# A planned order for attention and two MLPs on one core: fitted delays, backward passes, and the softmax bias moved to GpSimd

## The chip, the cores and the metric

One Trainium2 chip, one of its cores. The time is the device time of one execution in microseconds (us), the median of three runs. The engines are named as in the profile: PE (matrix multiply; PEld loads its stationary operand), DVE (VectorE), ACT (ScalarE), POOL (GpSimd), SP (here only the issuer of all the DMAs).

## What is computed

```python
mask = q_bucket[:, :, :, None] == k_bucket[:, :, None, :]   # 6 sign bits of q@proj and k@proj
scores = scale * np.matmul(q, k.transpose(0, 1, 3, 2))
scores = np.where(mask, scores, -1000000000.0)
scores = scores - np.max(scores, axis=-1, keepdims=True)
attn = np.exp(scores)
attn = attn / (np.sum(attn, axis=-1, keepdims=True) + 1e-09)
x = np.matmul(attn, v)                  # 2 batches, 8 heads, 768 x 64; then to 1536 x 512
h = x @ moe_w_in; g = np.maximum(h, 0.0) ** 2; x = g @ moe_w_out          # 512 -> 2048 -> 512
h = x @ moe2_w_in; g = np.maximum(0.01 * h, h); out = g @ moe2_w_out
```

The weights and inputs are of higher precision than one pass of PE keeps, so each product is made of three matmuls on a high and a low half of each operand (`three`), and much of the work of DVE, ACT and POOL is the making of these halves.

## The kernel before, in words

**Attention.** For each of the two batches there are 48 slots: four pairs of heads, two heads each, six blocks of 128 queries (`attention`, `slot`). A slot is a chain. PE makes the scores of 128 queries against 768 keys into PSUM with four matmuls (L712). DVE goes over them once, with a floor that stands for the mask, copies them to SBUF (tile `e`) and takes the row maximum with `accum_out` (L733; the trace shows this as a TENSOR_SCALAR_CACHE_REDUCE and a DVE_READ_ACCUMULATOR). Before, the maximum is written into an unused column of the same PSUM bank. From it a bias for exp is made, 128 x 1 numbers (tile `sm`): the maximum times a scale plus a constant. It is made by DVE (L739) or by ACT (L742), as the planner chooses. ACT takes exp in place (L745). Then `e` becomes a high half (ACT L774 or DVE L775) and a low half (POOL L778 or DVE L779), which a DMA transposes (L792); or, for every second slot of batch 0, PE transposes `e` into PSUM (L756), and ACT and DVE make the halves from there (L764, L767). PE sums with v (L813 to L815), DVE and ACT divide (L837 to L853).

The bank of scores (key `("s", r)`) is free for the next scores when its last reader is done. Before, that reader is the bias, as it reads the maximum out of the bank. Batch 0 turns over three such banks, which also hold PE's transposes; batch 1 has one, the other PSUM being used by the MLP. `e` has four buffers in batch 0 and two in batch 1.

**MLP.** The first layer of batch 0 (`group`, `up`, `down`) is put among the slots of batch 1. The first layer of batch 1 and the second layer of both follow it alone (`alone`, `quad`, which makes the up products with seven block products in place of eight; `down`). Weights are fetched as 64-bit numbers (`wide`), converted by three DVE instructions (L988, L992, L995), kept in DRAM as fp32 for the second use and halved (ACT L1009 or DVE L1010; POOL L1014).

**The order.** Nothing is scheduled by the framework: every step is handed to `Plan.do` with a due time, what it reads and writes, and one or more engines with a cost in us each (its choice of engines is ordered: the first is the preferred one). `Plan.order` then plays the steps through, engine by engine, in time order: of the steps that are ready on an engine it takes the one with the smallest due time, unless a step that prefers another engine would end sooner there (within MARGIN). A step is ready when what it depends on has ended, plus a delay: LAG between engines, LAND after a DMA, ISSUE before one. A cost marked `Port`, and every cost of POOL, takes a resource named `port`, one at a time: the SBUF access that DVE and POOL share. `weighed` mixes the due time that the kernel's text gives with one from the longest chain behind the step (OWN is the share of the former). The instructions are then issued on each engine's in-order queue in the order of the played times, and semaphores follow from the data. All DMAs go through the one queue of SP in that order. The due times come from constants (PITCH, MAX_AT, FETCH, ...).

Of the kernel before, what the change touches and what calls it, by code (L numbers as in the profile page):

```python
# [27 lines left out]
class Plan:  # L28
# [59 lines left out]
    def order(self):  # L88
        steps = self.weighed()
        left = [len(after) for _, after, _, _ in steps]  # L90
        users = [[] for _ in steps]
        for n, (_, after, _, _) in enumerate(steps):
            for a in after:
                users[a].append(n)
# [3 lines left out]
        end = {}  # L98
# [3 lines left out]

        def offer(n):
            _, after, ways, since = steps[n]
            for e in ways:
                t = since
                for a in after:
                    at, on = end[a]
                    if on == e:
                        lag = self.SAME.get(e, 0.12)  # L110
                    else:
                        lag = (self.LAND if on == "dma" else self.LAG) + (self.ISSUE if e == "dma" else 0.0)
                    t = max(t, at + lag)
                heapq.heappush(late[e], (t, n))
# [4 lines left out]
        while len(end) < len(steps):  # L119
# [40 lines left out]
            cost = steps[n][2][e][0]  # L160
# [10 lines left out]
        return [(n, e, t) for t, _, n, e in sorted(placed)]  # L171
# [3 lines left out]
def lsh_attention_moe_moe_kernel(  # L175
# [1423 lines left out]
```

## Time and profile before

| | us |
|---|---|
| median of 3 runs | 797.35 (792.97 to 799.29) |
| the profiled execution's own time | 799.07 |
| its span, first to last instruction | 797.3 |
| PE busy | 697.5, 87% of the span |
| DVE busy | 633.4, 79% |
| ACT busy | 501.7, 63% |
| POOL busy | 257.6, 32% |
| mean granted clock of PE, as a share of 2.4 GHz | 0.959 |

The span divides by what PE is doing: attention of batch 0 until about 156 us, then a hand-over until 182 in which the MLP's first products begin; attention of batch 1 with the first MLP layer of batch 0 until about 384; a second hand-over until about 435; then the MLP alone to the end. The profile's busy times are sums of durations. On DVE and ACT the next instruction may start some hundredths of a microsecond before the last has ended, so the distance between starts is a little less than a duration. A wait is written "engine line <- engine tile line: us, times, longest".

### The profile page before, as it was taken

The page shows a single profiled execution, that of the slowest core. Times are in us where ns is not written, and L with a number is a line of the kernel's source. Part 1 is how long each engine was busy: PE and PEld are TensorE (multiplying, and loading weights), DVE is VectorE, ACT ScalarE, POOL GpSimd, SP SyncE. Part 2 cuts the span into 40 slices and gives each one's busy share as a digit, 9 for nine tenths or more (in the row PEclk, how much of TensorE's full clock was granted, in tenths as well). Part 3 has the DMA queues.
Part 4 walks back from the last instruction along what each step waited for, and adds up shares of the span by engine and source line. Part 5 has one row for each costly group of instructions (what it writes and reads, how often), then busy time and mean ns, then how long its engine had stood idle before and what let it go on. Part 6 is the DMA issues. An engine that isn't in the chain of part 4 may idle for free.

```text
span 797.3 us, 14295 instructions
## 1 busy us (share of the span) xinstructions
PE 697.5 (87%) x5408; PEld 545.5 (68%) x5408; DVE 633.4 (79%) x1304; ACT 501.7 (63%) x938; POOL 257.6 (32%) x207
## 2 busy tenths in 40 slices
PE   3686757579996895899997999999899999999998
PEld 2474545478895794698973788787567666676776
DVE  7889898968888779799889987788988578567332
ACT  4888688648678569666869875554766545434320
POOL 2332234223445335634436842311121123012000
PEclk9899999869999898799999999999999999999999
DMA  3467778697999999998821241213123304201012
GB/s 119 89 157 153 211 147 153 124 254 146 224 246 199 177 230 178 243 239 196 187 80 61 73 131 55 80 53 106 30 77 106 106 1 138 74 0 54 14 53 92
DMA packets 185861, 100.81 MB, mean 126 GB/s; under 512 B 149440, under 2 KB 171968, under 8 KB 185792
## 3 DMA queue, kind: packets, MB, share of 16 engines
q1 hardware_dynamic: 185792, 99.90, 52.8%
q8 instruction: 42, 0.69, 0.4%
q14 instruction: 27, 0.22, 0.1%
HBM read 51.38 MB, written 11.53 MB: 79 GB/s over the span
## 4 chain that ended last, share of the span: by engine, by line
PE 67%; DVE 18%; DMA 5%; issue 4%; ACT 4%; POOL 0%; SPq 0%; DVEq 0%; ACTq 0%; POOLq 0%
PE acc L1075 19%; PE acc L1077 19%; PE acc L1076 19%; PE s L712 4%; DVE ep L733 3%; DMA wide<-in_moe_w_in_dram 2%; DVE xb L544 1%; PE av L813 1%; PE av L815 1%; PE av L814 1%; DMA rawk<-in_k_dram 1%; DVE lo L733 1%; DMA tt<-xb 1%; DMA part<-ep 1%; DVE xb L616 1%
## 5 line engine op out<-in xcount | busy, mean ns | idle before, releaser
L778 POOL TENSOR_TENSOR ep<-ep 128x768 f16<-128x768 f32 x30 | 50.6, 1686 | 85.2 <-ACT ep L774 74.2
L745 ACT ACTIVATE ep<-ep,sm,scs 128x768 f32<-128x768 f32 x60 | 61.6, 1027 | 22.3 <-DVE sm L739 19.8
L1075 PE MATMUL acc<-xa,wi 128*128 128x384 f32 x192 | 71.0, 370 | 0.0
L1075 PE MATMUL acc<-g,wo 128*128 128x384 f32 x192 | 69.4, 361 | 0.0
L1075 PE MATMUL acc<-xb,tt 128*128 128x384 f16 x192 | 63.8, 332 | 6.1 <-ACT xb L1022 2.3
L1077 PE MATMUL acc<-xb,tt 128*128 128x384 f16 x192 | 63.8, 332 | 2.5 <-DVE tt L1027 2.5
L1305 DVE TENSOR_TENSOR part<-acc,part 128x384 f32<-128x384 f32 (+1 forms) x66 | 38.5, 589 | 34.5 <-PE acc L1077 34.3
L1077 PE MATMUL acc<-xa,wi 128*128 128x384 f32 x192 | 65.9, 343 | 0.0
L1076 PE MATMUL acc<-xa,wi 128*128 128x384 f32 x192 | 65.7, 342 | 0.0
L1076 PE MATMUL acc<-g,wo 128*128 128x384 f32 x192 | 64.8, 337 | 0.0
L1077 PE MATMUL acc<-g,wo 128*128 128x384 f32 x192 | 64.8, 337 | 0.0
L1156 ACT ACTIVATE acc<-acc,small 128x384 f32<-128x384 f32 x48 | 26.5, 551 | 60.8 <-PE acc L1077 60.1
L1076 PE MATMUL acc<-xb,tt 128*128 128x384 f16 x192 | 63.5, 331 | 0.7 <-DVE xb L1027 0.7
L1014 POOL TENSOR_TENSOR wo<-w,wo 128x512 fp32r<-128x512 f32 x29 | 41.5, 1444 | 57.9 <-ACT wo L1009 31.8
L1014 POOL TENSOR_TENSOR wi<-w,wi 128x512 fp32r<-128x512 f32 x26 | 35.3, 1361 | 65.0 <-ACT wi L1009 63.1
L733 DVE TENSOR_SCALAR_CACHE_REDUCE ep<-s 128x768 f32<-128x768 f32 x48 | 45.8, 954 | 12.5 <-PE s L712 9.3
L1053 POOL TENSOR_TENSOR rawk<-w 128x256 f32<-128x256 f32 x15 | 13.7, 914 | 114.5 <-DVE tt L1027 78.1
L995 DVE SCALAR_TENSOR_TENSOR w<-wide,w 128x512 int32<-128x512 int32 x64 | 49.3, 775 | 0.3
L1075 PEld LDWEIGHTS <-tt 128*128 128x128 f16 x288 | 28.3, 98 | 29.4 <-issue 12.9
L1166 DVE TENSOR_TENSOR g<-acc,g 128x384 fp32r<-128x384 f32 x68 | 37.0, 549 | 12.3 <-ACT g L1161 12.3
L992 DVE SCALAR_TENSOR_TENSOR w<-wide,w 128x512 int32<-128x512 int32 x64 | 46.5, 733 | 0.4
L712 PE MATMUL s<-xb 128*128 128x384 f16 x144 | 33.0, 356 | 13.5 <-ACT sm L742 10.3
(316 smaller groups left out, 2414.6 us busy)
## 6 DMA issues: line engine op xcount, KB each, us to landing
wide<-in_moe_w_in_dram SPq DMA_DIRECT2D x32, 512.0 KB, 4.7
w<-w SPq DMA_DIRECT2D x64, 256.0 KB, 2.9
wide<-in_moe_w_out_dram SPq DMA_DIRECT2D x32, 512.0 KB, 4.2
rawq<-in_q_dram SPq DMA_DIRECT2D x8, 384.0 KB, 3.7
rawk<-in_k_dram SPq DMA_DIRECT2D x8, 384.0 KB, 3.9
rawv<-in_v_dram SPq DMA_DIRECT2D x8, 384.0 KB, 4.2
out_dram<-part SPq DMA_DIRECT2D x6, 256.0 KB, 2.0
out_dram<-xtok SPq DMA_DIRECT2D x6, 256.0 KB, 2.0
```

Of the source, the lines that this page charges most:

```text
L712: nc.tensor.matmul(out=ps[:, j, :HALF], lhsT=t[x][:, 0, n, :], rhs=t[x][:, 1, h * NTB + j * HB:h * NTB + (j + 1) * HB, :].rearrange("p n c ...
L733: nc.vector.tensor_scalar(out=e.rearrange("p (a c) -> p a c", a=2), in0=s_tile(r)[:, :, :HALF], scalar1=FLOOR, scalar2=None, op0=ALU.max, ...
L745: do(d + EXP_AT, [smk, ("scs", x3)] + early, ek, act=(1.03, lambda: nc.scalar.activation(out=e, in_=e, func=ACTF.Exp, scale=scs[x3][:, 0:1 ...
L778: pool=(1.65, lambda: nc.gpsimd.tensor_tensor(out=p[:, 1, :], in0=e, in1=p[:, 0, :], op=ALU.subtract)),
L992: (Port(0.6), lambda: nc.vector.scalar_tensor_tensor(out=oi, in0=t[:, :, 0], scalar=29, in1=oi, op0=ALU.logical_shift_right, op1=ALU.bitwi ...
L995: (Port(0.6), lambda: nc.vector.scalar_tensor_tensor(out=oi, in0=t[:, :, 1], scalar=-0x40000000, in1=oi, op0=ALU.bitwise_and, op1=ALU.bitw ...
L1014: eng.tensor_tensor(out=lo, in0=o, in1=hi.bitcast(FP32), op=ALU.subtract)
L1075: nc.tensor.matmul(out=acc, lhsT=st[0], rhs=mv[0], start=first, stop=False, skip_group_check=skip)
L1076: nc.tensor.matmul(out=acc, lhsT=st[0], rhs=mv[1], start=False, stop=False, skip_group_check=skip)
L1077: nc.tensor.matmul(out=acc, lhsT=st[1], rhs=mv[0], start=False, stop=last, skip_group_check=skip)
L1166: eng.tensor_tensor(out=gl, in0=src(), in1=gh.bitcast(FP32), op=ALU.subtract)
L1305: do(d, [key] + yk, yk, dve=(0.15 + n * 0.00105, lambda: nc.vector.tensor_tensor(out=yp(), in0=bank()[:, :n], in1=yp(), op=ALU.add)))
```

## The change

Three parts. (1) The row maximum goes into a tile of its own in SBUF (`top`, four buffers) instead of a column of the PSUM bank, so the bias no longer reads the bank. (2) The bias is made by POOL, or by DVE where the planner so chooses; ACT no longer makes it, and the constant tile `ln1024` goes. (3) The planner: `LAND`, `LAG` and `ISSUE` give way to delays by engine (`SAME`, `LAG`, `INTO`); the costs of some forty kinds of step and the constants of due times are changed; and `order` plays the steps three times forward, with a backward play between them. The backward play takes the ends of a forward play as its due times and starts from the last step, and the times that it finds are the due times of the next forward play. The order of the forward play that ends first in the planner's own count is kept. The arithmetic and the steps are otherwise the same.

The core of the diff (left out: further changed costs of the same kind as those shown, the removed tile's memset and the call of `Plan` with ROUNDS):

```diff
 
-    SAME = {"pe": 0.0, "dma": 0.0}
-    LAND = 2.0
-    LAG = 0.27
-    ISSUE = 1.0
-
-    def __init__(self, margin, own):
+    SAME = {"pe": 0.0, "dma": 0.0, "act": 0.13, "dve": 0.11, "pool": 0.08}
+    LAG = {"pe": 0.2, "dve": 0.12, "act": 0.14, "pool": 0.1, "dma": 2.4}
+    INTO = {"pe": 0.0, "dve": 0.0, "act": 0.0, "pool": 0.04, "dma": 0.05}
+
+    def __init__(self, margin, own, rounds):
         self.margin = margin
         self.own = own
+        self.rounds = rounds
         self.steps = []
         self.writer = {}
         self.readers = {}
@@ -77,7 +77,7 @@
             rest[n] += ways[e][0]
             for a in after:
                 on = next(iter(steps[a][2]))
-                lag = 0.12 if on == e else (self.LAND if on == "dma" else self.LAG) + (self.ISSUE if e == "dma" else 0.0)
+                lag = self.SAME[e] if on == e else self.LAG[on] + self.INTO[e]
                 rest[a] = max(rest[a], rest[n] + lag)
         whole = max(rest)
         return [
@@ -85,13 +85,13 @@
             for n, (due, after, ways, since) in enumerate(steps)
         ]
 
-    def order(self):
-        steps = self.weighed()
-        left = [len(after) for _, after, _, _ in steps]
-        users = [[] for _ in steps]
-        for n, (_, after, _, _) in enumerate(steps):
-            for a in after:
-                users[a].append(n)
+    def run(self, due, after, ways, since, back):
+
+        users = [[] for _ in due]
+        left = [len(a) for a in after]
+        for n, a in enumerate(after):
+            for m in a:
+                users[m].append(n)
         engines = ("pe", "dve", "act", "pool", "dma")
         free = dict.fromkeys(engines, 0.0)
         port = 0.0
@@ -100,23 +100,23 @@
         ready = {e: [] for e in engines}
         placed = []
 
+        def lag(first, then):
+            if first == then:
+                return self.SAME[then]
+            return self.LAG[first] + self.INTO[then]
+
         def offer(n):
-            _, after, ways, since = steps[n]
-            for e in ways:
-                t = since
-                for a in after:
+            for e in ways[n]:
+                t = since[n]
+                for a in after[n]:
                     at, on = end[a]
-                    if on == e:
-                        lag = self.SAME.get(e, 0.12)
-                    else:
-                        lag = (self.LAND if on == "dma" else self.LAG) + (self.ISSUE if e == "dma" else 0.0)
-                    t = max(t, at + lag)
+                    t = max(t, at + (lag(e, on) if back else lag(on, e)))
                 heapq.heappush(late[e], (t, n))
 
         for n, k in enumerate(left):
             if not k:
                 offer(n)
-        while len(end) < len(steps):
+        while len(end) < len(due):
             best = None
             for e in engines:
                 while late[e] and late[e][0][1] in end:
@@ -135,20 +135,20 @@
             while late[e] and late[e][0][0] <= t:
                 _, n = heapq.heappop(late[e])
                 if n not in end:
-                    heapq.heappush(ready[e], (steps[n][0], n))
+                    heapq.heappush(ready[e], (due[n], n))
             passed = []
             while ready[e]:
-                due, n = heapq.heappop(ready[e])
+                d, n = heapq.heappop(ready[e])
                 if n in end:
                     continue
-                passed.append((due, n))
-                first = next(iter(steps[n][2]))
+                passed.append((d, n))
+                first = next(iter(ways[n]))
                 if first == e:
                     break
 
-                queue = sum(steps[m][2][first][0] for d, m in ready[first] if m not in end and d <= due and m != n)
-                over = max(free[first], t) + queue + steps[n][2][first][0]
-                if t + steps[n][2][e][0] + self.margin < over:
+                queue = sum(ways[m][first][0] for x, m in ready[first] if m not in end and x <= d and m != n)
+                over = max(free[first], t) + queue + ways[n][first][0]
+                if t + ways[n][e][0] + self.margin < over:
                     break
             else:
                 n = None
@@ -157,7 +157,7 @@
             if n is None:
                 free[e] = t + 0.1
                 continue
-            cost = steps[n][2][e][0]
+            cost = ways[n][e][0]
             if e == "pool" or isinstance(cost, Port):
                 t = port = max(t, port)
                 port += cost
@@ -168,7 +168,30 @@
                 left[u] -= 1
                 if not left[u]:
                     offer(u)
-        return [(n, e, t) for t, _, n, e in sorted(placed)]
+        return placed
+
+    def order(self):
+        steps = self.weighed()
+        due, after, ways, since = ([s[x] for s in steps] for x in range(4))
+        users = [[] for _ in steps]
+        for n, a in enumerate(after):
+            for m in a:
+                users[m].append(n)
+        best = None
+        for _ in range(self.rounds):
+            placed = self.run(due, after, ways, since, False)
+            at = {n: (t, e) for t, _, n, e in placed}
+            whole = max(t + ways[n][e][0] for n, (t, e) in at.items())
+            if best is None or whole < best[0]:
+                best = (whole, placed)
+            over = {n: {e: ways[n][e]} for n, (t, e) in at.items()}
+            back = self.run(
+                [whole - at[n][0] - over[n][at[n][1]][0] for n in range(len(steps))],
+                users, over, [0.0] * len(steps), True,
+            )
+            for t, _, n, e in back:
+                due[n] = -t - over[n][e][0]
+        return [(n, e, t) for t, _, n, e in sorted(best[1])]
...
     BY_PE = 2
-    PE_LAG = 4.14
-    SECOND = -3.48
+    PE_LAG = 4.78
+    SECOND = -4.30
     VLATE = -5.50
-    OWN = 0.30
+    OWN = 0.27
     FIN_ACT = 1
     SQ_ACT = 2
-    MARGIN = 0.58
-    MAX_AT = 3.18
-    EXP_AT = 0.62
-    HI_AT = 2.36
-    LO_AT = -4.03
+    ROUNDS = 3
+    MARGIN = 0.71
+    MAX_AT = 2.33
+    EXP_AT = -0.37
+    HI_AT = 2.65
+    LO_AT = -3.85
     TURN_AT = -2.86
-    DONE_AT = -5.94
-    PREP_AT = -0.71
-    PREP_STEP = 0.42
-    LAG0 = -4.16
-    FETCH = 14.94
-    CONVERT = 6.27
-    KEEP = -11.40
-    AGAIN = 23.41
-    FETCH0 = 2.44
-    LEAD0 = 55.19
-    CONVERT0 = -3.65
+    DONE_AT = -7.24
+    PREP_AT = 1.57
+    PREP_STEP = 0.34
+    LAG0 = -4.44
+    FETCH = 14.86
+    CONVERT = 6.32
+    KEEP = -4.78
+    AGAIN = 25.52
+    FETCH0 = 0.22
+    LEAD0 = 49.60
+    CONVERT0 = -2.88
     LOAD1_AT = -19.15
-    HALVE = 9.81
+    HALVE = 13.02
     T_UP = 4096.0
-    SIZE16 = 2.73
+    SIZE16 = 1.85
...
-    ln1024 = tensor("ln1024", [128, 1])
+    top_ = [tensor(f"top{r}", [128, 1]) for r in range(4)]
...
-        sm = sm_[ring("sm", 4)]
-        smk = ("sm", turns["sm"] % 4)
+        z = ring("sm", 4)
+        sm, smk, top, topk = sm_[z], ("sm", z), top_[z], ("top", z)
         early = [] if b else ["given"]
         (e, ek), half, (pt, ptk) = rings_of(b, i)
-
-        top = ("top", r)
 
         def maximum():
             nc.vector.tensor_scalar(
                 out=e.rearrange("p (a c) -> p a c", a=2), in0=s_tile(r)[:, :, :HALF], scalar1=FLOOR, scalar2=None,
-                op0=ALU.max, op1=ALU.max, accum_out=s_tile(r)[:, 1, HALF:HALF + 1],
-            )
-
-        do(d + MAX_AT, [("s", r)] + extra + early, [top] + ek, dve=(1.09, maximum))
-        do(d + MAX_AT + 0.1, [("s", r), top, ("scs", x3)] + extra, [smk], dve=(0.22, lambda: nc.vector.tensor_scalar(
-            out=sm, in0=s_tile(r)[:, 1, HALF:HALF + 1], scalar1=scs[x3][:, 1:2], scalar2=LN1024,
-            op0=ALU.mult, op1=ALU.add,
-        )), act=(0.24, lambda: nc.scalar.activation(
-            out=sm, in_=s_tile(r)[:, 1, HALF:HALF + 1], func=ACTF.Identity, scale=scs[x3][:, 1:2], bias=ln1024,
-        )))
-        do(d + EXP_AT, [smk, ("scs", x3)] + early, ek, act=(1.03, lambda: nc.scalar.activation(
+                op0=ALU.max, op1=ALU.max, accum_out=top,
+            )
+
+        def bias(eng):
+            eng.tensor_scalar(
+                out=sm, in0=top, scalar1=scs[x3][:, 1:2], scalar2=LN1024, op0=ALU.mult, op1=ALU.add
+            )
+
+        do(d + MAX_AT, [("s", r)] + extra + early, [topk] + ek, dve=(0.88, maximum))
+        do(
+            d + MAX_AT + 0.1, [topk, ("scs", x3)], [smk],
+            pool=(0.24, lambda: bias(nc.gpsimd)), dve=(0.13, lambda: bias(nc.vector)),
+        )
+        do(d + EXP_AT, [smk, ("scs", x3)] + early, ek, act=(0.93, lambda: nc.scalar.activation(
...
-        do(d + HI_AT, ek + early, hk, act=(0.83, lambda: nc.scalar.copy(out=p[:, 0, :], in_=e)),
+        do(d + HI_AT, ek + early, hk, act=(0.72, lambda: nc.scalar.copy(out=p[:, 0, :], in_=e)),
            dve=(Port(0.47), lambda: nc.vector.tensor_copy(out=p[:, 0, :], in_=e)))
         do(
             d + LO_AT, ek + hk + early, lk,
-            pool=(1.65, lambda: nc.gpsimd.tensor_tensor(out=p[:, 1, :], in0=e, in1=p[:, 0, :], op=ALU.subtract)),
+            pool=(1.61, lambda: nc.gpsimd.tensor_tensor(out=p[:, 1, :], in0=e, in1=p[:, 0, :], op=ALU.subtract)),
...
-            dma=(1.78 * m + 0.47, lambda: nc.sync.dma_start_transpose(
+            dma=(1.78 * m + 0.05, lambda: nc.sync.dma_start_transpose(
...
-    PITCH = 1.89
+    PITCH = 1.74
     LEAD = 9.06
-    START = 13.54
-    MLP_OFF = 10.91
+    START = 13.68
+    MLP_OFF = 6.30
     MLP_AT = START + N_ATT * PITCH + MLP_OFF
-    STRETCH = 2.19
-    AT1_OFF = -0.28
+    STRETCH = 1.89
+    AT1_OFF = -1.43
     AT1 = MLP_AT + AT1_OFF
-    PITCH1 = 3.85
-    PREP1_AT = -14.00
-    PREP1_STEP = 5.97
-    COLD = 1.05
+    PITCH1 = 3.11
+    PREP1_AT = -9.57
+    PREP1_STEP = 6.76
+    COLD = 1.25
...
-            do(d, [("s", 0)], [("s", 0, "a"), ("s", 0, "b")], dve=(0.0, lambda: None))
+            do(d, [], [("s", 0), ("s", 0, "a"), ("s", 0, "b")], dve=(0.0, lambda: None))
```

## Rows read from the trace of the kernel before

**Rows 1.** The page, part 1: busy us, share of the span, instructions
```profile
PE 697.5 (87%) x5408; PEld 545.5 (68%) x5408; DVE 633.4 (79%) x1304; ACT 501.7 (63%) x938; POOL 257.6 (32%) x207
```

**Rows 2.** Windows by stage: us, busy us of PE, PEld, DVE, ACT, POOL; clock, DMA
```profile
20.00:156.00 136.00, 92.66 (x1310) 70.37 (x1309) 123.24 (x289) 111.27 (x174) 44.59 (x27) 0.95 0.69 146
156.00:182.00 26.00, 19.96 (x149) 16.96 (x148) 17.44 (x42) 11.04 (x22) 5.18 (x4) 0.67 0.85 223
182.00:384.00 202.00, 178.87 (x1715) 156.86 (x1714) 177.36 (x360) 147.77 (x250) 95.63 (x62) 0.93 1.01 212
384.00:435.00 51.00, 44.56 (x288) 35.15 (x287) 45.12 (x88) 40.31 (x95) 23.26 (x20) 0.98 0.34 91
435.00:797.00 362.00, 354.16 (x1890) 260.67 (x1888) 255.74 (x474) 181.46 (x384) 83.03 (x75) 0.99 0.22 70
```

**Rows 3.** The chain that ended last: shares of the span by engine
```profile
PE 67%; DVE 18%; DMA 5%; issue 4%; ACT 4%; POOL 0%; SPq 0%; DVEq 0%; ACTq 0%; POOLq 0%
```

**Rows 4.** Tile sm: the bias, durations ns min/median/max, first and last start us
```profile
L739 DVE TENSOR_SCALAR sm<-s,scs x40: 189/204/220, 41.7 to 372.0; 128x1 f32<-128x1 f32 x40
L742 ACT ACTIVATE sm<-s,ln,scs x32: 332/351/363, 22.3 to 380.6; 128x1 f32<-128x1 f32 x32
L739 DVE TENSOR_SCALAR sm<-sx,scs x16: 190/209/220, 23.8 to 149.1; 128x1 f32<-128x1 f32 x16
L742 ACT ACTIVATE sm<-sx,ln,scs x8: 334/350/358, 26.5 to 126.7; 128x1 f32<-128x1 f32 x8
```

**Rows 5.** Windows of line L739 alone: us, busy us of DVE (instructions), clock, DMA
```profile
20.00:182.00 162.00, 5.97 (x29) 0.91 0.72 159
182.00:384.00 202.00, 5.41 (x27) 0.93 1.01 212
```

**Rows 6.** Waits of PE ended by the bias in 182 to 384: us, times, longest
```profile
PE s L712 <- ACT sm L742: 10.3, 6, 3.3
...
PE s L712 <- DVE sm L739: 1.2, 2, 0.7
```

**Rows 7.** Waits of PE ended by the bias in 20 to 182
```profile
PE s L712 <- ACT sm L742: 6.1, 5, 2.2
PE sx L712 <- ACT sm L742: 3.6, 3, 1.8
...
PE sx L712 <- DVE sm L739: 3.1, 2, 2.5
...
PE sx L756 <- DVE sm L739: 2.7, 1, 2.7
```

**Rows 8.** Timeline near 254: one bank of scores, from row maximum to next scores
```profile
253.72 0.95 DVE L733 TENSOR_SCALAR_CACHE_REDUCE ep<-s 128x768 f32<-128x768 f32 x1
...
254.60 0.14 DVE L733 DVE_READ_ACCUMULATOR ep<-s 128x1 f32 x1
...
255.30 0.35 ACT L742 ACTIVATE sm<-s,ln,scs 128x1 f32<-128x1 f32 x1
255.70 1.44 PE L712 MATMUL s<-xb 128*128 128x384 f16 x4 [3.30 <-ACT sm L742]
```

**Rows 9.** Groups of POOL: busy us, mean ns, idle before and releasers
```profile
L778 POOL TENSOR_TENSOR ep<-ep 128x768 f16<-128x768 f32 x30 | 50.6, 1686 | 85.2 <-ACT ep L774 74.2 <-DVE ep L775 8.0 <-DVE w L988 2.2
...
L1447 POOL COPY pjk<-p 64x6 f16<-64x6 f16 x3 | 1.0, 323 | 0.1
L1447 POOL COPY pjq<-p 64x6 f16<-64x6 f16 x3 | 0.5, 182 | 5.7 <-DVE p L1442 5.7
```

**Rows 10.** Timeline: one small DVE instruction alone, and beside a POOL subtraction
```profile
147.95 0.16 DVE L471 TENSOR_TENSOR sc<-am,targets 128x3 f32<-128x3 f32 x1
...
249.19 1.65 POOL L778 TENSOR_TENSOR ep<-ep 128x768 f16<-128x768 f32 x1
...
249.62 1.24 DVE L471 TENSOR_TENSOR sc<-am,targets 128x3 f32<-128x3 f32 x1
```

**Rows 11.** Waits of ACT for the bias over the whole span
```profile
ACT ep L745 <- DVE sm L739: 19.8, 13, 3.5
```

More of the change, by code (lines that the diff above doesn't have):

```diff
@@ L390, in w7_col @@
         return (lambda: ap()[:, at + cc * 128:at + (cc + 1) * 128]), keys
-    plan = Plan(MARGIN, OWN)
+    plan = Plan(MARGIN, OWN, ROUNDS)
     do = plan.do
@@ L429, in load @@
         src = {"q": q, "k": k, "v": v}[nm]
-        do(due, [], [("raw", nm)], since=since, dma=(1.25, lambda: nc.sync.dma_start(
+        do(due, [], [("raw", nm)], since=since, dma=(1.1, lambda: nc.sync.dma_start(
             out=raw[nm], in_=src[b, 2 * pr:2 * pr + 2].rearrange("h (p t) d -> p h t d", t=NTB)
@@ L461, in spread @@
             )
-        do(due, [rk], [rk], dve=(Port(0.25), spread))
+        do(due, [rk], [rk], dve=(Port(0.31), spread))
         do(due, [rk], tb, pe=(0.1, lambda: nc.tensor.matmul(
@@ L589, in turn_pe @@
                 ways = dict(reversed(ways.items()))
-            do(d, reads + extra, keys, pe=(0.65, fn))
+            do(d, reads + extra, keys, pe=(0.35, fn))
             do(
@@ L763, in slot @@
                 d + 3.6, [("s", y)] + extra + early, hk,
-                act=(0.78, lambda: nc.scalar.copy(out=to[:, 0], in_=s_tile(y)[:, :, :HALF])),
+                act=(0.69, lambda: nc.scalar.copy(out=to[:, 0], in_=s_tile(y)[:, :, :HALF])),
                 dve=(0.87, lambda: nc.vector.tensor_copy(out=to[:, 0], in_=s_tile(y)[:, :, :HALF])),
@@ L858, in finished @@
         scale = ("sc", x3)
-        do(d + DONE_AT, av + [scale], [("rd", half)], dve=(0.46, divisor))
+        do(d + DONE_AT, av + [scale], [("rd", half)], dve=(0.34, divisor))
         do(
             d + DONE_AT + 0.5, av + [("rd", half)], [("x", hh, tq // HB)],
-            **({"act": (0.93, divide_act), "dve": (0.28, divide)} if FIN_ACT else
-               {"dve": (0.28, divide), "act": (0.93, divide_act)})
+            **({"act": (0.6, divide_act), "dve": (0.28, divide)} if FIN_ACT else
+               {"dve": (0.28, divide), "act": (0.6, divide_act)})
         )
@@ L964, in weights @@
         if not fresh:
-            do(d - AGAIN, [kept], [ok], dma=(0.9, lambda: nc.sync.dma_start(out=o, in_=where)))
+            do(d - AGAIN, [kept], [ok], dma=(0.75, lambda: nc.sync.dma_start(out=o, in_=where)))
         else:
@@ L983, in weights @@
                 d - (FETCH0 if first else FETCH), [], [tk],
-                since=d - (LEAD0 if first else LEAD), dma=(1.70, fetch),
+                since=d - (LEAD0 if first else LEAD), dma=(1.45, fetch),
             )
@@ L999, in weights @@
             if L == 0:
-                do(d - KEEP, [ok], [kept], dma=(1.0, lambda: nc.sync.dma_start(out=where, in_=o)))
+                do(d - KEEP, [ok], [kept], dma=(0.75, lambda: nc.sync.dma_start(out=where, in_=o)))
         r = f % FG
@@ L1008, in weights @@
         given = ["given"] if kind == "o" else []
-        do(d - HALVE, [ok] + given, hk, act=(0.62, lambda: nc.scalar.copy(out=w_of(kind, r)[0], in_=o)),
+        do(d - HALVE, [ok] + given, hk, act=(0.51, lambda: nc.scalar.copy(out=w_of(kind, r)[0], in_=o)),
            dve=(Port(0.34), lambda: nc.vector.tensor_copy(out=w_of(kind, r)[0], in_=o)))
@@ L1034, in tall @@
         dump, dk = spot(f"raw{r % 2}", 2 * KB, DM, BF16)
-        do(d - SIZE16, [ok, "late"], dk + [("aw", r)], act=(0.63, lambda: nc.scalar.activation(
+        do(d - SIZE16, [ok, "late"], dk + [("aw", r)], act=(0.62, lambda: nc.scalar.activation(
             out=dump(), in_=o, func=ACTF.Abs, accum_out=aw[:, r:r + 1],
@@ L1052, in add @@
         def add(out, a, c, op, reads, writes, dx):
-            do(dx, reads, writes, pool=(0.8, lambda: nc.gpsimd.tensor_tensor(out=out(), in0=a(), in1=c(), op=op)),
-               dve=(0.5, lambda: nc.vector.tensor_tensor(out=out(), in0=a(), in1=c(), op=op)))
+            do(dx, reads, writes, pool=(0.7, lambda: nc.gpsimd.tensor_tensor(out=out(), in0=a(), in1=c(), op=op)),
+               dve=(Port(0.33), lambda: nc.vector.tensor_tensor(out=out(), in0=a(), in1=c(), op=op)))
         def half(f, x):
@@ L1160, in bent @@
         held_in_psum = key[0][0] == "acc"
-        do(d + 1.1, key + ["given"], gkey[:1], act=(0.51, lambda: nc.scalar.copy(out=g_of(r, j, y)[0], in_=src())),
-           dve=(0.55 if held_in_psum else Port(0.3), lambda: nc.vector.tensor_copy(out=g_of(r, j, y)[0], in_=src())))
+        do(d + 1.1, key + ["given"], gkey[:1], act=(0.37, lambda: nc.scalar.copy(out=g_of(r, j, y)[0], in_=src())),
+           dve=(0.47 if held_in_psum else Port(0.28), lambda: nc.vector.tensor_copy(out=g_of(r, j, y)[0], in_=src())))
         def low(eng):
@@ L1168, in bent @@
         do(d + 1.6, key + gkey[:1], gkey[1:], **(
-            dict(dve=(0.57, lambda: low(nc.vector))) if held_in_psum else
-            dict(dve=(Port(0.5), lambda: low(nc.vector)), pool=(1.1, lambda: low(nc.gpsimd)))
+            dict(dve=(0.47, lambda: low(nc.vector))) if held_in_psum else
+            dict(dve=(Port(0.47), lambda: low(nc.vector)), pool=(0.97, lambda: low(nc.gpsimd)))
         ))
@@ L1203, in quad @@
         product(E, "S1", "T1", True, d + us)
-        do(d + us, [A[0]], [B2[0]] + B2[1], act=(0.47, lambda: nc.scalar.copy(out=t(B2), in_=t(A))))
-        do(d + 2 * us, [E[0]], fk, act=(0.47, lambda: nc.scalar.copy(out=five(), in_=t(E))))
+        do(d + us, [A[0]], [B2[0]] + B2[1], act=(0.38, lambda: nc.scalar.copy(out=t(B2), in_=t(A))))
+        do(d + 2 * us, [E[0]], fk, act=(0.38, lambda: nc.scalar.copy(out=five(), in_=t(E))))
         acc_done(E[0])
@@ L1323, in spread @@
                 )
-            do(d - 1.0, ["sw", ("sx", b)], [("back", b)], dve=(Port(0.2), spread))
+            do(d - 1.0, ["sw", ("sx", b)], [("back", b)], dve=(Port(0.31), spread))
     def first_weights(L, g, d, stretch, source):
```

51 lines of the change are left out of this document (25 added, 26 removed).

## Prediction

> **What bounds the kernel now.** I read the page's busy times first, then windows cut where PE's work changes, the chain that ended last, the waits of PE, and the bias itself. PE is busy 697.5 of 797.3 us [rows 1] and holds 67% of the chain [rows 3], so the question is in which stretch anything else still holds the end. The windows say it [rows 2]. From 435 us on PE is busy 354.2 of 362 us: only fewer matmuls could shorten that, and the change takes none away. From 20 to 156 (attention, batch 0) PE is busy 92.7 of 136 us, DVE 123.2 and ACT 111.3: DVE bounds it, with 12.8 us idle. From 156 to 182 (hand-over to the MLP) every engine has holes and PE's granted clock is 0.67; the clock has two levels, 1.2 and 2.4 GHz, so a mean of 0.67 is 2 x 0.33 x 26 = 17 us at the lower. From 182 to 384 (attention of batch 1 among the first MLP layer) PE has 178.9 of 202 and DVE 177.4; neither alone bounds it, PE idles 23.1 us, and a clock of 0.93 is 28 us at the lower level. From 384 to 435 PE idles 6.4 us. So the change can win in the first 435 us, in DVE's load up to 156 and in PE's holes after that.
>
> **The bias leaves DVE and ACT.** In the traced run DVE made 40 + 16 = 56 biases of some 0.205 us and ACT 32 + 8 = 40 of 0.35 [rows 4]: 11.5 us of DVE and 14 us of ACT. DVE made 29 before 182 and 27 after [rows 5]. As it has almost no slack up to 156, the 29 are on the path, though each frees less than its duration, since the next instruction starts before it has ended: near 254 the accumulator's read starts 0.88 after a row maximum that lasts 0.95 [rows 8]. Their 6.0 us [rows 5] are the upper end, and 0 the lower, if all came back to DVE; I take 4. After it 5.4 us go from DVE [rows 5], which is no more the bound there than PE: I take 2 (0 to 5.4). ACT is busy 73 to 82% of the time in both: 0.
>
> **The bank of scores is free earlier.** The next scores wait now for the row maximum alone. Near 254 one sees what that is worth: the accumulator's read ended at 254.74, ACT began the bias at 255.30 because it was in other work, and PE, idle for 3.30 us, started at 255.70 [rows 8]. Without the bias it would have started about 0.96 us sooner; the rest of the 3.30 stays, because then the row maximum is late. In 182 to 384 there are 8 such waits, 11.5 us [rows 6]. At least ACT's own 0.35 or DVE's 0.2 goes from each (8 x 0.3 = 2.4), at most 0.96 (7.7); nearer to the low end, 3.5. From 20 to 182 there are 11, 15.5 us in all [rows 7], but PE is not the bound there, and what they give DVE is in its 4 us.
>
> **The bias arrives on POOL.** The trace shows POOL make no such thing. The nearest rows are copies of 64 x 6 at 182 and 323 ns [rows 9], against 205 and 350 ns for the bias now: the instruction by itself costs between 0.03 less and 0.12 more than on DVE. It adds one hand-over from DVE to POOL where the bias was on DVE; on ACT there was one already. What matters is the queue. POOL's other work comes in pieces of 1.69 us (L778 [rows 9]), and it is busy 33% of the time up to 156 and 47% from 182 to 384 [rows 2]. A bias that arrived blindly would find a piece running with these chances and wait half of it, 0.84 us: 48 x 0.33 x 0.84 = 13 us and 48 x 0.47 x 0.84 = 19 us, 32 in all, as the upper end. Queued behind the bias are the other subtractions; behind exp, the high half, the subtraction again, the transposing DMA on SP and the sums of PE, and in batch 1, with two buffers of `e`, the row maximum after next. That exp can be late is seen: ACT stood 19.8 us before it, in 13 waits, for a bias from DVE [rows 11]. But the planner knows POOL's pieces and places around them, and may give the bias to DVE. I take +2; the ends are -2 (ACT's and DVE's queues no longer in the way) and +32.
>
> The port is the second price. A 128 x 3 instruction of DVE that takes 0.16 us alone took 1.24 us when it started at 249.62 under a POOL subtraction of 249.19 to 250.84 [rows 10]. The biases of DVE, which read the maximum from PSUM, all keep within 189 to 220 ns [rows 4]. One that DVE makes from SBUF may now be held; one on POOL may hold a DVE instruction for its 0.18 to 0.32 us. At a fifth of 96 that is 3.5 to 6 us of DVE, within the 32. The Trainium skill (SBUF - State Buffer, "Who interferes with whom") tells of this as a lock: a DVE instruction in a two-port mode or with two SBUF inputs, and one of GpSimd, exclude each other, and whichever comes second waits the other out. The trace agrees: 249.62 + 1.24 = 250.86 is the end of POOL's subtraction. By that rule the row maximum, which reads PSUM, is never held; no run here shows one that writes its accumulator to SBUF.
>
> **The order.** The new delays and costs can't be priced one by one; they and the backward plays move nearly every step, SP's DMAs included: weight fetches, stores (due 11.4 us after their use before, 4.8 now) and transposes share its one queue. The delay of a DMA's consumer falls from 2.0 + 1.0 to 2.4 + 0.05 us where a DMA waits for another engine, so transposes are expected sooner. What could be had is bounded by the holes [rows 2]: DVE's 12.8 us up to 156; 6.0 us of PE idle and half of 17 us at the low clock up to 182; 23.1 - 11.5 = 11.6 us of PE idle not ended by the bias and half of 28 us up to 384; 6.4 after it. Together 12.8 + 14.5 + 25.6 + 6.4 = 59 us. The other end is a loss of the same kind as one hand-over, 14.5 us, where due times are off. The end up to 435 is the sum of many short waits, the longest classes of some 10 us [rows 6]; a better order takes some away and makes others. I take a fifth of the 59: -12.
>
> **Sum.** -4 - 2 - 3.5 + 2 - 12 = -19.5 against the profiled execution's own 799.07 (span 797.3 and 1.8 around it): 779.6. The median of the runs before lies 1.7 lower, at 797.35; the profiled run is within their spread, so I take 1 off for half of that difference and forecast **779 us**.
>
> **Rivals.**
> - *The order gives much more.* If half of the 59 us goes: 799.07 - 7.5 - 29.5 + 0 = 763. For it: in the hand-over at 156 all engines have holes at once, which only an order explains. Against: DVE at 91% before it leaves little room.
> - *No gain in the order.* The old order was already full where it counts, the new one moves waits about, and the change gives only its local parts, with the lower ends: 799.07 - 2.4 - 2 = 795 (or as much if most biases go to DVE, and the change does not do what it says). For it: DVE's 91% and PE's 89% are near what such chains allow; 435 to 797 stays as it is.
> - *POOL's queue sets exp, slower.* The bias stands behind subtractions, the row maximum after next waits for the late `e`, and DVE and PE with it. It decides once more than the gains of bias and bank, 9.5 us without any from the order, of the 32 us falls on the path, a third. With two thirds, and no gain from the order, 799.07 - 9.5 + 21 = 811. For it: POOL's 47%, and pieces of 1.69 us against a bias of 0.2. Against: POOL is placed by the planner, and its idle time before these pieces is 85.2 us [rows 9]. The Trainium skill (GPSIMD Engine Reference, "Engine selection") speaks for this rival: elementwise work belongs on VectorE, GpSimd being some two times slower with two inputs and about equal with one. Whether that holds for 128 x 1 no run here shows.
> - *A worse order.* The same 14.5 us lost as above: 799.07 - 7.5 + 14.5 = 806.
>
> **Numbers.** The forecast has 0.48, the larger gain 0.22, no gain in the order 0.16, POOL's queue 0.08, the worse order 0.06. About 1%, 8 us, is what a measurement of this kernel can tell from no change. Faster by over that (below 789): the first two, and a fifth of the third: 0.48 + 0.22 + 0.03 = 0.73. Slower (above 805): the last two but for 0.03, 0.11. Within: 0.13 + 0.03 = 0.16. For the range, the forecast's own is 770 to 789; to leave out no more than 2 in 10 it must reach past the larger gain, to 755, and past the case without gain, to 801.
>
> **What would show it.** Right: the row maximum writes `top`, the bias stands under POOL in most of 96 slots at 0.2 to 0.3 us, and no scores wait for `sm`; the MLP alone, some 360 us at 0.99, is as long as before and starts near 415 instead of 435; DVE up to the hand-over is busy a few us less. Wrong: ACT waiting before exp for POOL by more than the 20 us that it waits now for DVE; DVE instructions of 0.2 us grown to over 1 in greater number; a start of the MLP alone at 430 or later; or PE idle inside it, waiting for weights that SP fetched late.

## The result, and the profile after

The changed kernel takes 775.88 us (median of 4, 773.62 to 777.76) against 796.9 in the same comparison: a ratio of 0.974, interval 0.9691 to 0.9788. It is faster by 21 us; 779 was forecast. Ratios leave out runs that lie more than 1.5% above the fastest of the same kernel: two of ten in the first experiment, whose median without them is 791.4 us, and none elsewhere. The profiled execution took 776.67 us over a span of 774.9.

The page after, part 1 (against [rows 1]), and the shares of the chain that ended last:

```profile
PE 697.1 (90%) x5408; PEld 545.6 (70%) x5408; DVE 610.1 (79%) x1218; ACT 511.9 (66%) x970; POOL 294.3 (38%) x289
...
PE 42%; DVE 5%; ACT 5%; DMA 3%; issue 3%; POOL 1%; DVEq 0%; POOLq 0%; SPq 0%; ACTq 0%
```

PE is busy as long as before, 697.1 us against 697.5, so the whole difference of the spans, 22.4 us, is time in which PE stood idle: 99.8 us before, 77.8 after. The chain can't be set beside [rows 3]: its shares add up to 59% of the span, the other to 98%.

The same windows as in [rows 2], after (us; busy us of PE, PEld, DVE, ACT, POOL; clock; DMA; GB/s):

```profile
20.00:156.00 136.00, 99.89 (x1342) 75.37 (x1341) 126.43 (x273) 111.46 (x171) 53.56 (x67) 0.91 0.79 167
156.00:182.00 26.00, 23.45 (x172) 20.65 (x169) 18.75 (x46) 20.71 (x40) 10.36 (x10) 0.86 0.71 172
182.00:384.00 202.00, 182.84 (x1767) 161.04 (x1764) 170.25 (x325) 154.88 (x284) 121.37 (x101) 0.95 1.01 216
384.00:435.00 51.00, 47.16 (x280) 35.72 (x279) 43.62 (x83) 43.41 (x101) 28.10 (x24) 1.00 0.27 83
435.00:775.00 340.00, 334.61 (x1789) 246.39 (x1786) 236.07 (x441) 170.30 (x361) 74.89 (x68) 1.00 0.21 69
```

Fixed windows no longer hold the same work. Cut at two events, the start of the first MLP product and that of the last row maximum of batch 1, they do: the instruction counts of PE nearly agree. Before, then after:

```profile
0.00:171.40 171.40, 109.31 (x1473) 83.12 (x1474) 148.94 (x369) 125.98 (x196) 50.48 (x48) 0.93 0.69 153
171.40:379.60 208.20, 185.56 (x1724) 162.84 (x1722) 179.24 (x367) 149.97 (x255) 99.58 (x65) 0.92 0.98 209
379.60:797.30 417.70, 402.64 (x2222) 299.52 (x2218) 305.23 (x570) 225.76 (x488) 107.53 (x95) 0.99 0.24 74
```

```profile
0.00:161.60 161.60, 112.09 (x1474) 84.51 (x1474) 144.68 (x338) 126.29 (x195) 59.57 (x88) 0.92 0.74 164
161.60:361.40 199.80, 183.25 (x1707) 160.46 (x1705) 169.40 (x324) 155.87 (x278) 124.10 (x104) 0.95 1.01 215
361.40:774.90 413.50, 401.72 (x2233) 300.62 (x2231) 296.02 (x557) 229.77 (x498) 110.63 (x97) 0.99 0.25 75
```

Attention of batch 0 is 9.8 us shorter, attention of batch 1 among the MLP 8.4, the rest 4.2. DVE's load falls by 4.3 us in the first and 9.8 in the second stretch, POOL's rises by 9.1 and 24.5.

The bias after (tile `sm`; ns min/median/max), its group on POOL (busy, mean), and ACT's waits for it, which answer to [rows 4] and [rows 11]:

```profile
L761 POOL TENSOR_SCALAR sm<-top,scs x85: 264/266/1421, 20.4 to 359.3; 128x1 f32<-128x1 f32 x85
L761 DVE TENSOR_SCALAR sm<-top,scs x11: 184/203/216, 31.7 to 364.6; 128x1 f32<-128x1 f32 x11
```

```profile
L761 POOL TENSOR_SCALAR sm<-top,scs 128x1 f32<-128x1 f32 x85 | 42.0, 494 | 93.7 <-DVE ep L755 32.0 <-DVE lo L755 15.4 <-DVE lg L755 10.3
```

```profile
ACT ep L770 <- POOL sm L761: 13.2, 12, 3.9
...
ACT pt L770 <- POOL sm L761: 3.4, 2, 3.1
ACT ep L770 <- DVE sm L761: 3.1, 3, 1.5
```

POOL makes 85 of 96. Alone one takes 266 ns, but the mean is 494: some are held. ACT waits 13.2 + 3.4 + 3.1 = 19.7 us before exp, no more than the 25.3 before (19.8 in [rows 11], 5.5 more before the `pt` tile); and before, it also waited 15.5 us for row maxima of which it was to make the bias itself. No matmul waits for `sm` between 20 and 384 any more; before they did for 28.2 us ([rows 6, 7] and small ones).

### The profile page after: what moved, and what is told of

Same layout as the page of the kernel before. It is cut to its first block, busy times and chain, and to the rows that moved or that the text cites. A ratio compares the mean times of both kernels' runs of the same rounds, so it can differ in the third digit from the quotient of the medians.

```text
span 774.9 us, 14277 instructions
## 1 busy us (share of the span) xinstructions
PE 697.1 (90%) x5408; PEld 545.6 (70%) x5408; DVE 610.1 (79%) x1218; ACT 511.9 (66%) x970; POOL 294.3 (38%) x289
## 4 chain that ended last, share of the span: by engine, by line
PE 42%; DVE 5%; ACT 5%; DMA 3%; issue 3%; POOL 1%; DVEq 0%; POOLq 0%; SPq 0%; ACTq 0%
PE acc L1100 14%; PE acc L1102 14%; PE acc L1101 13%; DMA w<-w 1%; DMA pt<-ep 1%; DVE xb L1052 1%; DVE w L1017 1%; DVE w L1020 1%; DMA wide<-in_moe_w_out_dram 1%; DMA pt<-more 1%; ACT wo L1034 1%; ACT xa L1186 0%; DVE xa L1191 0%; DVE w L1013 0%; PE s L736 0%
## 5 line engine op out<-in xcount | busy, mean ns | idle before, releaser
L761 POOL TENSOR_SCALAR sm<-top,scs 128x1 f32<-128x1 f32 x85 | 42.0, 494 | 93.7 <-DVE ep L755 32.0
L1100 PE MATMUL acc<-xa,wi 128*128 128x384 f32 x192 | 73.9, 385 | 1.8 <-DVE part L1330 1.1
L770 ACT ACTIVATE ep<-ep,sm,scs 128x768 f32<-128x768 f32 x60 | 61.9, 1034 | 16.7 <-POOL sm L761 13.2
L1078 POOL TENSOR_TENSOR rawk<-w 128x256 f32<-128x256 f32 x16 | 15.8, 988 | 141.5 <-DVE tt L1052 85.3
L1102 PE MATMUL acc<-xa,wi 128*128 128x384 f32 x192 | 67.3, 351 | 0.0
L1101 PE MATMUL acc<-xa,wi 128*128 128x384 f32 x192 | 66.8, 348 | 0.0
L1100 PE MATMUL acc<-xb,tt 128*128 128x384 f16 x192 | 63.0, 328 | 3.8 <-ACT acc L1229 2.1
L1039 POOL TENSOR_TENSOR wi<-w,wi 128x512 fp32r<-128x512 f32 x31 | 43.8, 1416 | 58.5 <-ACT wi L1034 58.3
L1101 PE MATMUL acc<-xb,tt 128*128 128x384 f16 x192 | 62.6, 326 | 0.4 <-DVE xb L1052 0.4
L1102 PE MATMUL acc<-xb,tt 128*128 128x384 f16 x192 | 62.6, 326 | 0.0
L1039 POOL TENSOR_TENSOR wo<-w,wo 128x512 fp32r<-128x512 f32 x25 | 35.5, 1424 | 60.1 <-ACT wo L1034 48.7
L1017 DVE SCALAR_TENSOR_TENSOR w<-wide,w 128x512 int32<-128x512 int32 x64 | 54.0, 846 | 0.4
L1020 DVE SCALAR_TENSOR_TENSOR w<-wide,w 128x512 int32<-128x512 int32 x64 | 52.4, 821 | 0.7
L1013 DVE TENSOR_SCALAR w<-wide 128x512 int32<-128x512 int32 x64 | 37.8, 592 | 9.3 <-DMA wide<-in_moe_w_out_dram 5.7
```

The source lines that it names most:

```text
L761: eng.tensor_scalar(out=sm, in0=top, scalar1=scs[x3][:, 1:2], scalar2=LN1024, op0=ALU.mult, op1=ALU.add)
L770: do(d + EXP_AT, [smk, ("scs", x3)] + early, ek, act=(0.93, lambda: nc.scalar.activation(out=e, in_=e, func=ACTF.Exp, scale=scs[x3][:, 0:1 ...
L1013: (Port(0.34), lambda: nc.vector.tensor_scalar(out=oi, in0=t[:, :, 1], scalar1=3, scalar2=0x3FFFFFF8, op0=ALU.logical_shift_left, op1=ALU. ...
L1017: (Port(0.6), lambda: nc.vector.scalar_tensor_tensor(out=oi, in0=t[:, :, 0], scalar=29, in1=oi, op0=ALU.logical_shift_right, op1=ALU.bitwi ...
L1020: (Port(0.6), lambda: nc.vector.scalar_tensor_tensor(out=oi, in0=t[:, :, 1], scalar=-0x40000000, in1=oi, op0=ALU.bitwise_and, op1=ALU.bitw ...
L1039: eng.tensor_tensor(out=lo, in0=o, in1=hi.bitcast(FP32), op=ALU.subtract)
```

## The experiments

Each group of runs has its own runs of the kernel before on the same chip, so ratios to it are compared; one hundredth is 8 us. Two kinds of kernel are used. In the first the steps are planned anew; in the second the order of every other instruction is kept as it stands in one of the two kernels, and only the bias or the place of the row maximum is changed. They are numbered e1 to e12 in the order in which they were run. The letters A to D in the expectations are theories of what carries the gain.

**The new order kept, the bias taken off POOL.** At the issue, the bias follows its row maximum on DVE (where the scales of its heads are already there; else at its place). PE, ACT and SP keep their orders instruction for instruction.

```diff
-        for n, e, _ in plan.order():
-            plan.steps[n][2][e][1]()
+        for n, e, _ in plan.order():
+            for x in (n, n + 1):
+                if x in gone or x > n and (x not in biases or not gone.issuperset(plan.steps[x][1])):
+                    continue
+                plan.steps[x][2]["dve" if x in biases else e][1]()
+                gone.add(x)
```

Expected of e1:

> The changed kernel's order of PE, ACT and SP kept instruction for instruction; only the bias is taken off POOL and put on DVE right behind its row maximum (85 instructions move). Theory A (the order carries most of the 21 us, the bias little): DVE's 6 us come back, POOL's 2 us go, so 778 to 782. Theory B (the bias on POOL carries most): 785 to 792. Theory C (POOL's queue delays exp and costs more than it frees): 768 to 774, faster than the changed kernel.

793.16 us, ratio 0.9928 (0.9896 to 0.996), which is 0.019 or 15 us over the changed kernel's 0.974: B's range, not A's. Its windows, cut at the same events:

```profile
0.00:174.80 174.80, 115.85 (x1473) 85.14 (x1474) 154.87 (x383) 127.55 (x195) 42.73 (x43) 0.89 0.67 152
174.80:377.50 202.70, 183.45 (x1707) 159.92 (x1705) 176.56 (x365) 155.56 (x278) 102.47 (x64) 0.95 1.00 213
377.50:791.10 413.60, 400.70 (x2235) 299.45 (x2233) 297.54 (x557) 230.02 (x498) 110.69 (x97) 1.00 0.25 75
```

13.2 us are lost in the first stretch, 2.9 in the second, none in the third. DVE's load in the first grew by 10.2 us, about what the 45 biases that came to it there take at 0.214 (9.6). ACT waited no longer for the bias than in the changed kernel (16.8 us against 17.8 + 3.8), so the loss is not in exp's wait. DVE is the busiest engine of this stretch, with 154.9 of 174.8 us, and in this order the bias on DVE cost its full load or more; PE's granted clock fell too, from 0.92 to 0.89. This is more than the 4 us of the prediction, but it is the price in an order that had no place for these biases on DVE.

The second kernel also puts the row maximum back into PSUM:

```diff
-                op0=ALU.max, op1=ALU.max, accum_out=top,
+                op0=ALU.max, op1=ALU.max, accum_out=s_tile(r)[:, 1, HALF:HALF + 1],
```

Expected of e2:

> As e1, and the row maximum is written back into the PSUM bank, so that the scores wait for the bias again. Theory A: another 3 to 4 us over e1, by the bank that is held longer, 781 to 786 in all. Theory B (the bank freed early carries much): 790 or more. If the bank is worth nothing: the same as e1 within 2 us.

797.35 us, 1.0001 (0.9977 to 1.0025): another 0.0073, 5.8 us, for the bank that is held and the slower read of the accumulator (141 ns in place of 82, below). In the traces 6.0 us are lost before the first MLP product (180.8 in place of e1's 174.8), none from there to the last row maximum (200.9 in place of 202.7), and 2.5 behind it.

**One pass, and the old planner with the new bias.**

```diff
-    ROUNDS = 3
+    ROUNDS = 1
```

Expected of e3:

> ROUNDS = 1: the order of the first forward play, no backward play, everything else as changed. If the passes carry the gain of the order (some 12 us): 785 to 792. If the fitted delays and constants carry it: 774 to 780. The MLP alone (from 435 on) keeps its length in both.

798.75 us, 1.0025 (1.0003 to 1.0047), outside both ranges. The next is the kernel before with the change's maximum and bias, at the old cost of the maximum:

```diff
+        do(d + MAX_AT, [("s", r)] + extra + early, [topk] + ek, dve=(1.09, maximum))
+        do(
+            d + MAX_AT + 0.1, [topk, ("scs", x3)], [smk],
+            pool=(0.24, lambda: bias(nc.gpsimd)), dve=(0.13, lambda: bias(nc.vector)),
+        )
```

Expected of e4:

> The kernel before with its own planner, delays and constants; only the row maximum in SBUF and the bias on POOL or DVE are added, and the old planner orders them. Theory A: the local parts alone, 4 + 2 + 3.5 - 2 = 7.5 us under before, 788 to 792. Theory B: 776 to 782. Theory C: 800 or more.

811.17 us, 1.0183 (1.0146 to 1.0221): slower than before, which neither A nor B allowed. It is C's number, but the trace does not show C's cause: ACT waited 34.1 us for the bias, against 27.6 before and the 15.5 for row maxima. Taken one by one every part of the change seems to carry all of the gain, and the bias alone to lose. Either the parts need each other, or any other order loses: theory D.

**The fourth corner, and neighbours of the changed kernel.** First the changed planner with the old maximum and bias; then two kernels in which one number of the planner moves by 0.01, and nothing that is computed.

```diff
+        do(d + MAX_AT, [("s", r)] + extra + early, [top] + ek, dve=(0.88, maximum))
+        do(d + MAX_AT + 0.1, [("s", r), top, ("scs", x3)] + extra, [smk], dve=(0.13, lambda: nc.vector.tensor_scalar(
...
```

Expected of e5:

> The changed planner, its passes, delays and constants; row maximum in PSUM and bias on DVE or ACT as before, planned anew (their costs 0.13 and 0.24). It is the fourth corner beside before (old planner, old bias), e4 (old planner, new bias) and the change. Theory A (planner carries it, parts add up): 780 to 786. Theory B (bias carries it): 793 to 800. Theory D (the gain belongs to one tuned point, its constants fitted to this very program, and every other program of the same planner loses it): 785 to 800, and e6 and e7 lose as much.

782.55 us, 0.9809 (0.9759 to 0.9858), in A's range.

```diff
-    MARGIN = 0.71
+    MARGIN = 0.70
```

Expected of e6:

> The changed kernel with MARGIN 0.70 in place of 0.71, nothing else: an order that differs in a few choices of engine and what follows from them. Theories A and B: within 3 us of 776. Theory D: 780 to 795, the scatter of the planner.

795.84 us, 0.9986 (0.9958 to 1.0014), just above D's range.

```diff
-    OWN = 0.27
+    OWN = 0.28
```

Expected of e7:

> The changed kernel with OWN 0.28 in place of 0.27: the due times of the first forward play move a little. Theories A and B: within 3 us of 776. Theory D: 780 to 795.

787.6 us, 0.9884 (0.9837 to 0.993), again D's. A hundredth in MARGIN costs 0.0246, 19.6 us, nearly all of the gain, and one in OWN 11.5. The changed kernel is one good point of its planner, and single kernels planned anew show little by being some 10 us off.

**The passes alone.** The kernel before with the change's `run` and `order` and three rounds, but its own delays:

```diff
+            if first == then:
+                return self.SAME.get(then, 0.12)
+            return (self.LAND if first == "dma" else self.LAG) + (self.ISSUE if then == "dma" else 0.0)
```

Expected of e8:

> The kernel before with its delays, costs, constants and bias; only the backward and forward plays are added. If the passes help by themselves: 785 to 792. If they need the fitted delays and costs: 797 or more. Theory D: anywhere between 785 and 810.

805.17 us, 1.0109 (1.005 to 1.0167): no gain from the passes by themselves, or D's scatter.

**Neighbours of the kernel before.** If it is such a point too, its neighbours must lose as well, and the two planners can be compared away from their best points.

```diff
-    MARGIN = 0.58
+    MARGIN = 0.57
```

Expected of e11:

> The kernel before with MARGIN 0.57 in place of 0.58. Theory D (both kernels are single tuned points of their planners, and a neighbour loses 10 to 20 us on either side): 803 to 815. If only the changed kernel is such a point: 795 to 800.

809.08 us, 1.0136 (1.0093 to 1.0179).

```diff
-    OWN = 0.30
+    OWN = 0.31
```

Expected of e12:

> The kernel before with OWN 0.31 in place of 0.30. Theory D: 803 to 815, so that the new planner's neighbours (796 and 788) stand as far below the old one's as the two kernels themselves. If only the changed kernel is a tuned point: 795 to 800, and the new planner is then no better than the old one away from it.

818.07 us, 1.0244 (1.0203 to 1.0286), 3 us above D's range. Both lose, 10.8 and 19.5 us. The neighbours of before have a mean ratio of 1.0190, those of the changed kernel 0.9935: 0.0255 or 20 us apart, as far as the two kernels, and the ranges don't meet. Two neighbours of each are few, and each constant was moved one way only; as far as they go, the difference belongs to the change and not to the choice of one point. Measured against its neighbours, e4 (1.0183) shows no effect of the bias, e8 (1.0109) 6 us for the passes, and e3 (1.0025 against 0.9935) 7 us for them from the other side. All three lie within the scatter of the planner, about 4 us either way among two neighbours, so 6 to 7 us for the passes is a hint that two runs share, and the rest of the 20, which goes to delays, costs, constants, bias and bank together, was not divided by these runs.

One piece of the gain does not scatter. The last 1700 instructions of PE take 329.2 to 330.6 us in all traces with the old delays, costs and constants (before, e4, e8 to e12) and 325.0 to 326.2 in all with the new ones (after, e1, e2, e3, e5 to e7). It comes with the passes or without them (e8 has the passes and not this gain, e3 the gain with one pass), and with either bias (e4, e5). So some 4 us of the 21 go to the delays, costs and constants. They lie in one place: in the old plans PE waits 2.2 or 2.3 us for a half of `xb`, and in before the granted clock around it is 0.96, in after 1.00. Before, that wait and its stretch, then the matching 200 instructions of PE after:

```profile
PE acc L1075 <- ACT xb L1022: 2.3, 1, 2.3
```

```profile
553.30:596.80 43.50, 39.71 (x201) 26.13 (x199) 39.39 (x75) 27.87 (x54) 10.29 (x11) 0.96 0.19 58
```

```profile
534.80:573.90 39.10, 37.87 (x202) 25.23 (x200) 35.74 (x71) 29.05 (x59) 10.04 (x9) 1.00 0.26 81
```

**The old order kept, the bias moved.** Two kernels keep the order of before on every engine. The first writes the maximum to SBUF and leaves the bias where it was; the second also issues every bias on POOL.

```diff
-                op0=ALU.max, op1=ALU.max, accum_out=s_tile(r)[:, 1, HALF:HALF + 1],
+                op0=ALU.max, op1=ALU.max, accum_out=top_at,
...
-            out=sm, in0=s_tile(r)[:, 1, HALF:HALF + 1], scalar1=scs[x3][:, 1:2], scalar2=LN1024,
+            out=sm, in0=top_at, scalar1=scs[x3][:, 1:2], scalar2=LN1024,
```

Expected of e9:

> The kernel before with its order kept on every engine; only the row maximum goes to SBUF and the bias, on the engine that it had, reads it there. That is the bank freed early and nothing else. By the prediction's term: 3.5 us less than before (2.4 to 7.7), 790 to 795. If an order planned for the old release can't use it: within 2 us of before.

793.17 us, 0.9949 (0.9922 to 0.9976): 4.1 us less, 1.9 to 6.2. The trace gains 3.2 us before the first MLP product (168.2 in place of 171.4), where DVE's load falls by 2.1, and 3.2 from there to the last row maximum. PE's waits for the bias between 20 and 384, 28.2 us before, are down to two, and where scores were next in line PE now waits for the row maximum itself, as the prediction had it:

```profile
PE s L713 <- DVE ep L735: 6.0, 6, 2.5
...
PE sx L758 <- DVE sm L741: 4.6, 1, 4.6
```

```diff
+        def bias():
+            nc.gpsimd.tensor_scalar(
+                out=sm, in0=top_at, scalar1=scs[x3][:, 1:2], scalar2=LN1024, op0=ALU.mult, op1=ALU.add
+            )
...
+        do(d + MAX_AT + 0.1, [("s", r), top, ("scs", x3)] + extra, [smk], dve=(0.22, bias), act=(0.24, bias))
```

Expected of e10:

> As e9, and all 96 biases are issued by POOL at the place in the order that they had on DVE or ACT; nothing is planned anew. By the prediction's terms (4 + 2 + 3.5 - 2): 788 to 792. If POOL's queue, not planned for the bias, makes exp late: 800 or more.

823.61 us, 1.0326 (1.0291 to 1.0361): 26 us slower than before and 0.0377, 30 us, slower than e9. ACT's waits show where:

```profile
ACT ep L747 <- POOL sm L741: 75.4, 49, 3.7
...
ACT pt L747 <- POOL sm L741: 10.7, 6, 4.4
...
ACT lo L747 <- POOL sm L741: 7.3, 5, 2.7
...
ACT lg L747 <- POOL sm L741: 3.4, 4, 1.4
```

96.9 us in 64 waits. In e9 ACT waited 43.2 us for the bias or, where it made the bias itself, for the row maximum (43.1 in the kernel before); in the changed kernel 21.6. Issuing the bias on POOL in an order that does not know of it costs 30 us; in the order made for it, taking it off POOL costs 15 (e1). Neither is the price of the move where both places are planned; the one pair of plans for that, e5 and the changed kernel, lies 5.5 us apart, which is within the scatter.

## Why the prediction was right

**What bounds it.** Right. The busy time of PE is the same in sum, so all that was won lies in its idle time, and 18.2 of 22.4 us before the last row maximum of batch 1. The MLP alone was to start near 415 in place of 435 and to keep its length. Measured by the work of the prediction's last window, which is the last 1890 instructions of PE [rows 2], it does: it starts 19.2 us sooner. Before, then after:

```profile
434.60:797.30 362.70, 354.56 (x1891) 260.87 (x1889) 256.14 (x474) 181.86 (x385) 83.44 (x75) 0.99 0.22 70
```

```profile
415.40:774.90 359.50, 352.20 (x1892) 259.94 (x1889) 254.32 (x464) 189.80 (x405) 90.24 (x79) 1.00 0.22 71
```

The 3.2 us by which it is shorter, which the prediction put at nothing, come with the piece that does not scatter (above).

**The bank: -3.5 (2.4 to 7.7).** The size is right: 4.1 us in the old order (e9), 5.8 in the new one (e2 to e1). The place is right only in part, and the cause is not separated. The prediction looked for the gain from 182 to 384 and gave the bank nothing of its own in batch 0. In the traces half of e9's gain and most of e2's loss lie before the first MLP product. Both runs also change the accumulator's read by 59 ns, which the prediction did not have; it is 2.8 us of DVE's load in either batch, and no run parts it from the freed bank.

**The bias off DVE: -4 and -2, and POOL +2.** Neither the parts nor the sum are shown, and nothing contradicts the sum. Of the changed planner with and without the new bias and bank, 0.9809 and 0.974, the difference is 5.5 us, with intervals that overlap and between two plans that may scatter by more; 7.5 was forecast for these three terms and the bank together. In the new order, kept, DVE's 10.2 us of biases in batch 0 cost 13.2 us (e1), more than "4 of 6" would have it. The value of -4 came from 29 biases on DVE and 19 on ACT, as the old planner shared them; e5 had 76 on DVE and 20 on ACT and lost only the 5.5, so a new plan seems to pay for them elsewhere.

**POOL's queue: rival at 811.** The mechanism is real: a bias that arrives blindly costs 30 us (e10). That 32 had been reckoned is luck, for that was the sum of the waits of all 96 biases. In e10 they start 146.3 us in sum behind their accumulator reads, in e9 50.1, so they wait 96 us more; of that some 54 reach ACT and 30 the end. In the changed kernel the sum is 39.8, and ACT's waits before exp fell instead of rising. The rival's condition, an order not made for the bias, did not hold.

**The order: -12.** Right in sign, and by these runs too small. The changed planner with the old bias is 15 us under before (0.9809); the neighbours of both, bias and bank included, are 20 apart. What the prediction did not have at all is the scatter: a share (OWN) or a margin moved by a hundredth cost 10 to 20 us, for the kernel before as for the changed one. Its rivals "no gain in the order" and "a worse order", at 795 and 806, are not far from what the same planner gave at other points: e6 795.84, and with one pass e3 798.75. With such a scatter, a forecast within 3 us is partly luck. (The sum for the larger gain, 799.07 - 7.5 - 29.5, is 762, not 763.)

**The signs.** "No scores wait for `sm`" and "DVE busy a few us less up to the hand-over" (148.9 to 144.7) hold. "At 0.2 to 0.3 us" holds for the median of POOL's bias, not the mean. DVE instructions of at most three elements per partition that took over 1 us fell from 8 to 3, and PE waited for no DMA inside the MLP alone. The row maxima, which now write their maximum to SBUF, took 928 to 959 ns and were not held. The fear that DVE's bias, now read from SBUF, would be held did not come true: all 96 of them in e1 took 212 to 217 ns, 33 of these wholly under a subtraction on POOL.

## What to carry to other kernels

A hand-made or searched order is a point: before crediting a part of a change with a gain, run neighbours of either kernel that compute the same, two at least, and keep the order fixed where one instruction's place is in question. A piece of the gain that stands in every plan of one kind and in none of the other, as the 4 us above, can be read from the traces without more runs. An instruction on an engine with idle time is not free if that engine's queue is in order: 0.27 us on POOL cost 30 us behind pieces of 1.65 us where its place was not planned, and where POOL's was planned and DVE's was not, the move away from it cost 15. A small result that one engine reads for another is worth a look at the buffer that it keeps busy.

## What the runs showed of the hardware

The accumulator's read is faster into SBUF than into PSUM. Before and after (ns min/median/max):

```profile
L733 DVE DVE_READ_ACCUMULATOR ep<-s x48: 129/141/144, 182.7 to 380.4; 128x1 f32 x48
```

```profile
L755 DVE DVE_READ_ACCUMULATOR ep<-s x48: 74/82/86, 170.3 to 362.3; 128x1 f32 x48
```

The other runs agree: 140 or 141 ns wherever the maximum goes to PSUM (e2, e5, e8, e11, e12), 81 to 83 wherever it goes to SBUF. 59 ns times 96 is 5.7 us of DVE. ACT's bias went the other way: 351 ns when it reads PSUM [rows 4], and in e9 386 ns from SBUF:

```profile
L744 ACT ACTIVATE sm<-top,ln,scs x40: 364/386/393, 20.8 to 374.2; 128x1 f32<-128x1 f32 x40
```

The port holds POOL's bias, not DVE's. The longest of POOL's 85, in the changed kernel's timeline:

```profile
311.56 0.96 DVE L804 TENSOR_TENSOR ep<-ep 128x768 f16<-128x768 f32 x1 [0.18 <-ACT ep L799]
312.44 0.69 DVE L1020 SCALAR_TENSOR_TENSOR w<-wide,w 128x512 int32<-128x512 int32 x1
```

```profile
311.75 1.42 POOL L761 TENSOR_SCALAR sm<-top,scs 128x1 f32<-128x1 f32 x1
```

It starts under a DVE subtraction with two SBUF operands and ends at 313.17, 0.04 after the second of the two DVE instructions: it waited both out. The Trainium skill (SBUF - State Buffer, "Who interferes with whom") says that such a DVE instruction and a GpSimd instruction that reads SBUF exclude each other, and that one with at most one SBUF input, outside the two-port modes, does not contend with GpSimd. This trace agrees with the first; e1's 212 to 217 ns agree with the second, though no run shows in which mode so small an instruction ran. Over 85 biases the holding comes to 42.0 - 85 x 0.266 = 19.4 us of POOL's time: 37 of them took over 0.3 us, each beside a DVE instruction whose operands all lie in SBUF.
